# Gated mix of linear attention and a GEGLU MLP: changes of the moving side as own streams, values split when made, the first handover spread over two units

## The chip, the cores and the metric

The kernel runs on one core of one Trainium2 chip. The metric is the device time of one execution in microseconds (us). The kernel before takes 2434.32 us, the median of three runs (2431.76 to 2439.18).

## The reference

Two branches on the same tokens x (2048 x 1024) are mixed by a gate per token:

```python
g = sigmoid((x * gate_w).sum(-1, keepdims=True))
# a: hedgehog linear attention, 32 heads of 32
q, k, v = split(x @ wqkv)
phi(t) = concat(softmax(t @ w_phi), softmax(-(t @ w_phi)))     # per head
kv = einsum("bhsf,bhsd->bhfd", phi(k), v);  z = phi(k).sum over tokens
a = (phi(q) @ kv / (phi(q) @ z + 1e-6)) @ wo
# b: GEGLU MLP, 1024 -> 3584 -> 1024
b = (gelu(x @ w_gate) * (x @ w_up)) @ w_down
out = g * a + (1 - g) * b
```

## The kernel before

Every product is made in fp32 accuracy out of fp32r parts: each operand is split into a high part (a copy, by ScalarE, ACT) and a low part (a subtraction, by VectorE, DVE), and three passes (PASSES) of matmuls run for each pair. A 2x2 block product takes seven products instead of eight, of sums and differences of the blocks, which DVE makes. One such set is a **unit**: two row blocks of a weight matrix (the right operands x, y, z and v) against a quarter of a moving side (operands x and s). A unit has seven slots, and `product` (L680) issues twelve matmuls in each; `unit` ends and moves the banks of PSUM, and `results` passes the four result blocks on.

There are 79 units after the start: 1–7 for the values v, 8–15 for the keys k, 16–47 for queries q, gates g and ups u of one half of the tokens, and 48–79 for those of the other half (g and u alternate, the four q units stand between them). The first v unit is made plainly in the **start** (L267), straight from the raw wv and x blocks. w_phi is folded into the k weights by 16 **folds** (`fold_piece`, L287) right behind it and into the q weights by 16 more (L793). An out stage (L1369), which the change leaves alone, follows the last unit.

Where a group of units ends, the moving side changes (`change_half`): seven operands of four pieces are loaded by SyncE's DMA queue (SP), split by ACT and DVE and put into their place between the last use of the old and the first use of the new. This happens before unit 8 (the moving side becomes the folded k weights), unit 16 and unit 48 (the two halves of x).

Beside the units run: `key_sums` (sums of the folded k weights, stored for the first change), `gates` (the token gates), `features` (32 jobs: phi of a block of keys, split values, and the accumulation L913 into kv), `finish_z` (sums of phi over tokens) and `attention` (32 jobs: phi of queries, L1113, and the division). Results travel through DRAM: v and k rows by `store_rows`, queries, and the left operands la and lm of the out stage.

The order of all this is planned by hand when the kernel is built. Each helper is a generator that yields an earliest slot, a latest slot and its costs on DVE and ACT; `run_slot` picks, behind the twelve matmuls of each slot, those that are due or fit into the planned clocks of both engines. `fillers` are small groups of matmuls that are put behind a product. Each engine then works its own list strictly in that order, and so do the DMA queues of SP and of GpSimd (POOL), which carry loads and stores. The planner's numbers are fixed ones; what really takes longer makes the engine behind it wait.

Buffers set the rest: `stage` has three, `tyz` three (y and z of two units), `h` (`hidden`) three for results on their way out, `w0` four quarters (`gated`), `misc` two banks of PSUM.

The lines around the accumulation and the changes read:

```python
for h in range(2):
    high(vs[h][:, :, 0], pv[:, h])
yield now[0], NEVER, 0.75
for h in range(2):
    low(vs[h][:, :, 1], pv[:, h], vs[h][:, :, 0])
if after:
    load("v", work[:, 0], *after)
```

Of the kernel before, what the change touches and what calls it, by code (L numbers as in the profile page):

```python
# [16 lines left out]
P = 128  # L17
# [16 lines left out]
def tile_gated_mix(ctx: ExitStack, tc: tile.TileContext, x, xT, wkT, wqT, wv, w_phi, wo,  # L34
# [74 lines left out]
    tokens = {k: [dram.tile([NG, P, 4, P], F32, name=f"{k}t{b}") for b in range(S // BLK)] for k in "kv"}  # L109
# [44 lines left out]

    def store_chunk(m, i, k, t):
# [14 lines left out]
    with tc.manual_schedule(engines={PE, DVE, ACT, SP}):  # L170
# [22 lines left out]
        def plain_weights(s, n):  # L193
            k = kcs[s]
            for f in range(2):
                nc.scalar.dma_start(pieces[s // 4][:, s % 4:s % 4 + n, f * P:f * P + P],
                                    xT3[:, k:k + 4 * n - 3:4, f * BLK:f * BLK + P])
# [4 lines left out]
        nc.scalar.dma_start(phi_c, w_phi.rearrange("(g h) d f -> (h d) g f", h=4))  # L202
# [37 lines left out]
        for s in range(KC):  # L240
# [17 lines left out]
            if s == 3:  # L258
                for h in range(2):
                    t = fp.tile([P, 4, 4, 32], F32, tag=f"vs{h}", name="bp", bufs=1)  # L260
# [12 lines left out]
        rooms.append(new_work(0))  # L273
        homes = [t[:, n] for t, many in zip(rooms, (2, 2, 4)) for n in range(many)]
        homes.append(fa.tile([P, BLK], F32, tag="o2", name="fold", bufs=1))
        homes += homes[2:]
# [6 lines left out]
        def fold_piece(i):  # L283
# [7 lines left out]
            if 5 <= i < 12:  # L291
                fold_load(i + 4)

        for i in range(9):
            fold_load(i)
        results_0 = new_work(1)
# [9 lines left out]
        def plain_out(n, j, f):  # L306
            high(results_0[:, n], plain_banks[j, f])
            store_rows("v", 0, 1 - f, j, results_0[:, n])

        sum_steps(100)  # L310
        fold_piece(0)
        plain_out(0, 1, 0)
        fold_piece(1)
        plain_out(1, 0, 1)
        high(flat(x1)[0], first_e)
        low(flat(x1)[1], first_e, flat(x1)[0])
        fold_piece(2)
        plain_out(2, 0, 0)
        quarter_sums(first_e, first_o, True)
        high(flat(y1)[0], first_o)  # L320
        fold_piece(3)
        plain_out(3, 1, 1)
        low(flat(y1)[1], first_o, flat(y1)[0])
        x_splits = [(k, 0) for k in range(4)] + [(0, kc) for kc in range(1, 4)] + [(k, kc) for k in range(1, 4) for kc in range(1, 4)]
        x_highs, x_lows = zip(*[sum_parts(k, kc) for k, kc in x_splits])
        x_highs, x_lows = list(x_highs), list(x_lows)

        def more(n, m):
            for _ in range(n):
                x_highs.pop(0)()  # L330
            for _ in range(m):
                x_lows.pop(0)()

        more(2, 0)
        fold_piece(4)
        more(2, 4)
        fold_piece(5)
        more(3, 3)
        more_sums(first_e, first_o, True)
        z1 = slot()  # L340
        high(flat(z1)[0], first_e)
        fold_piece(6)
        low(flat(z1)[1], first_e, flat(z1)[0])
        more(9, 9)
# [69 lines left out]
        def key_sums(pa):  # L414
            for kc in range(KC // 2):
# [6 lines left out]
                for k in (kc - 1, kc):  # L422
                    r1, r2 = wide if k % 2 else [pa[:, 0], pa[:, 1]]
                    four = a11, a12, a21, a22 = r1[:, :BLK], r1[:, BLK:], r2[:, :BLK], r2[:, BLK:]
                    yield now[0], NEVER, 2.8
                    for _ in w_steps(*four):
                        pass
# [4 lines left out]
        def gates(pa):  # L432
            rows = [pa[:, 1], *wide]
            nc.sync.dma_start(pa[:, 0], gate_w[None, :].to_broadcast([P, D]))

            def load(c):
                nc.sync.dma_start(rows[c % 3], x[c * P:(c + 1) * P, :])
# [3 lines left out]
            for c in range(3):  # L441
                load(c)
            for c in range(S // P):
                r = rows[c % 3]
# [3 lines left out]
                if c + 3 < S // P:  # L448
                    load(c + 3)
# [6 lines left out]
        def change_half(t, half):  # L456

            b = 2 * half
            if half == 1:
# [8 lines left out]
            many = 2 if half == 3 else 1  # L468
            parts = [(i, j, t + free + 1, t + need) for i, free, need in order for j in range(0, 4, many)]
            if half < 3:  # L470
                homes = [gated(1, 0), *((gated(0, 0), gated(0, 1)) if half == 2 else (e2[:, 0], e2[:, 1]))]
            else:
                while not free[0]:
                    yield now[0] + 1, NEVER, 0.0
                free[0] = False
                raw = xa.tile([P, 2, 2 * BLK], F32, tag="pts", name="raw", bufs=1)
                homes = [raw[:, 0], raw[:, 1], *wide]
            N, H = len(parts), len(homes)
            TAIL = N if half < 3 else N - 6
            at = [n % H if n < TAIL else n % 2 for n in range(N)]  # L480

            def load(n):
                i, j, _, _ = parts[n]
                nc.sync.dma_start(homes[at[n]].rearrange("p (a b) -> p a b", a=many), srcs[i][:, j:j + many, :])

            loaded = [0]

            def more(n):
                while loaded[0] < N and (loaded[0] < H or any(at[m] == at[loaded[0]] for m in range(loaded[0] - H, n))):
                    if any(at[m] == at[loaded[0]] for m in range(n, loaded[0])):  # L490
                        break
                    load(loaded[0])
                    loaded[0] += 1

            def pieces(ns):
                for n in ns:
                    i, j, last, need = parts[n]
                    x = homes[at[n]].rearrange("p (a b) -> p a b", a=many)
                    yield max(now[0], last), need - 2, 0.0, 1.05 * many / 2
                    if j == 0 and i in (0, 3, 6):  # L500
                        q = ((b + 1, 0), (b + 1, 1), (b, 1))[i // 3]
                        xb[q] = new_quarter(*q)
                    q = [x_operands(half)[i][:, a, j:j + many, :] for a in range(2)]
                    high(q[0], x)
                    yield now[0], need - 1, 1.25 * many / 2
                    low(q[1], x, q[0])
                    more(n + 1)

            more(0)
            yield from pieces(range(TAIL))  # L510

            def tail():
                yield from pieces(range(TAIL, N))
                free[0] = True

            if TAIL < N:
                start(tail())
# [3 lines left out]
        for half in (2, 3):  # L521
            mine = [(half, k, m) for m in range(NF // 2) for k in "gu"]
# [7 lines left out]
        def weights(n, half, kind, m):  # L530
# [12 lines left out]
            if n == 1:  # L543
                mine.update(x=x1, y=y1, z=z1)
# [98 lines left out]
        gate_parts = []  # L643

        def gated(j, m):
            if not gate_parts:
                gate_parts.append(new_work(0))
# [15 lines left out]
        def plain_results(kind, half, m):  # L663
            def out(j, odd, x, t):
# [4 lines left out]
                else:  # L669
                    store_rows(kind, m, odd, j, t)  # L670
# [740 lines left out]
```

## Time and profile before

| what | us |
|---|---|
| median of three runs | 2434.32 (2431.76 to 2439.18) |
| the profiled execution | 2431.56 |
| its span | 2429.7 |
| TensorE (PE) busy | 2353.8 |
| DVE busy | 1759.0 |
| ACT busy | 1212.8 |
| GpSimd (POOL) busy | 364.5 |

In the trace a row of the timeline has the start, the duration, the engine, the line, the operation, the tiles (out<-in) with their shapes, and in brackets the idle time before it and what released it. ACTq and SPq are the engines' DMA queues. A row of a table by stretches has the stretch, its length, and for each engine the busy time with the count of instructions, then the granted TensorE clock (1.00 is full), the busy share of the DMA engines and the GB/s that they moved. A row of the waits has what waited and for what, the sum, the count and the longest. A row of DMA issues has the count, the size and the median time from issue to landing.

### The profile page before, as it was taken

The numbers are of one execution on the slowest core, as the hardware profiler recorded it, in microseconds if no ns is written. First come the engines' busy times: TensorE is split into PE (matmuls) and PEld (weight loads), VectorE is DVE, ScalarE is ACT, GpSimd is POOL, SyncE is SP. The second block draws the span as 40 slices with busy tenths as digits, with TensorE's granted clock in tenths as the row PEclk, the third lists the DMA queues.
The fourth block names the chain that finished last, engine by engine and source line by source line (L and its number), as shares of the span: only waits on it lengthen the run. The fifth ranks groups of instructions, "written<-read, shape, count | busy, mean of one in ns | idle before, by whom it ended". The sixth has DMA issues, their size and how long they took to land. (4 is left out here: it accounts for less than half of the span.)

```text
span 2429.7 us, 29400 instructions
## 1 busy us (share of the span) xinstructions
PE 2353.8 (97%) x10414; PEld 1931.5 (79%) x10414; DVE 1759.0 (72%) x2391; ACT 1212.8 (50%) x1706; POOL 364.5 (15%) x585
## 2 busy tenths in 40 slices
PE   7999999999999999999999899999999999999999
PEld 6777786788787777777778788888888888888887
DVE  6665456788987788856788788787375678877873
ACT  4335445565655555643777677777344222323221
POOL 1122331222221222211111111111000000000000
PEclk8999999999999999999999999999999999999999
DMA  7887678778887888897778778787786667887774
GB/s 244 277 269 254 231 247 277 281 280 299 298 286 259 285 270 285 278 358 281 234 244 266 230 252 270 244 262 242 248 302 216 234 216 267 311 288 280 269 272 139
DMA packets 243556, 640.70 MB, mean 264 GB/s; under 512 B 31680, under 2 KB 72400, under 8 KB 227024
## 3 DMA queue, kind: packets, MB, share of 16 engines
q1 hardware_dynamic: 183616, 428.14, 52.1%
q0 software_dynamic: 56544, 209.50, 25.2%
q8 instruction: 82, 1.34, 0.2%
q10 hardware_dynamic: 3248, 1.18, 0.2%
q14 instruction: 66, 0.54, 0.1%
HBM read 428.47 MB, written 210.51 MB: 263 GB/s over the span
## 5 line engine op out<-in xcount | busy, mean ns | idle before, releaser
L1369 PE MATMUL po<-tw,wgu 128*128 128x512 f32 x1344 | 309.8, 389 | 0.0
L56 ACT ACTIVATE wgu<-stage 128x1024 fp32r<-128x1024 f32 (+2 forms) x168 | 174.6, 1040 | 240.9 <-DVE stage L1259 160.8
L1369 PEld LDWEIGHTS po<-tw,wgu 128*128 128x128 f32 x1344 | 252.3, 188 | 52.4
L680 PE MATMUL b<-s,tyz 128*128 128x512 f32 x936 | 233.2, 397 | 13.9 <-ACT b L726 7.3
L680 PE MATMUL a<-s,tyz 128*128 128x512 f32 x948 | 233.8, 395 | 11.6 <-DMA tyz<-tu0z 3.7
L680 PE MATMUL p<-s,tyz 128*128 128x512 f32 x936 | 228.6, 393 | 8.6 <-DVE tyz L59 5.8
L680 PE MATMUL a<-s,v 128*128 128x512 f32 x948 | 232.9, 394 | 3.9 <-ACT s L56 3.1
L680 PE MATMUL a<-x,wgu 128*128 128x512 f32 x948 | 233.1, 395 | 2.8 <-DVE w L693 2.8
L59 DVE TENSOR_TENSOR wgu<-stage,wgu 128x1024 fp32r<-128x1024 f32 (+2 forms) x136 | 162.7, 1196 | 101.0 <-ACT wgu L56 100.0
L680 PE MATMUL c<-x,tyz 128*128 128x512 f32 x948 | 231.1, 392 | 2.3 <-ACT x L56 0.9
L680 PE MATMUL c<-x,wgu 128*128 128x512 f32 x948 | 230.0, 391 | 0.1
L680 PEld LDWEIGHTS b<-s,tyz 128*128 128x128 f32 x936 | 176.2, 190 | 58.2 <-ACT b L726 10.6
L680 PEld LDWEIGHTS a<-s,tyz 128*128 128x128 f32 x948 | 178.3, 190 | 52.9 <-issue 7.1
L680 PEld LDWEIGHTS p<-s,tyz 128*128 128x128 f32 x936 | 175.7, 189 | 49.7 <-DVE tyz L59 7.3
L680 PEld LDWEIGHTS a<-x,wgu 128*128 128x128 f32 x948 | 180.9, 192 | 42.5 <-DVE w L693 3.9
L680 PEld LDWEIGHTS a<-s,v 128*128 128x128 f32 x948 | 178.2, 190 | 43.0 <-ACT s L56 4.8
L680 PEld LDWEIGHTS c<-x,tyz 128*128 128x128 f32 x948 | 177.8, 189 | 41.9 <-ACT c L711 2.8
L680 PEld LDWEIGHTS c<-x,wgu 128*128 128x128 f32 x948 | 178.7, 189 | 38.0 <-DVE x L59 0.8
L56 ACT ACTIVATE tyz<-stage 128x1024 fp32r<-128x1024 f32 x95 | 100.2, 1055 | 120.8 <-DVE stage L134 118.4
L1369 PE MATMUL po<-tw,wl 128*128 128x512 f32 x672 | 156.9, 389 | 0.0
L1369 PE MATMUL po<-tyz,wgu 128*128 128x512 f32 x672 | 155.2, 389 | 0.0
L1369 PEld LDWEIGHTS po<-tw,wl 128*128 128x128 f32 x672 | 126.1, 188 | 26.2
(318 smaller groups left out, 3614.1 us busy)
## 6 DMA issues: line engine op xcount, KB each, us to landing
stage<-lm SPq DMA_DIRECT2D x98, 512.0 KB, 4.5
sr<-in_w_down SPq DMA_DIRECT2D x84, 512.0 KB, 5.0
sl<-lm SPq DMA_DIRECT2D x70, 512.0 KB, 4.8
lm<-h POOLq DMA_DIRECT2D x112, 256.0 KB, 5.8
stage<-in_w_gate SPq DMA_DIRECT2D x42, 512.0 KB, 7.1
stage<-in_w_up SPq DMA_DIRECT2D x42, 512.0 KB, 5.6
zs<-w POOLq DMA_DIRECT2D x32, 512.0 KB, 6.0
la<-h POOLq DMA_DIRECT2D x64, 256.0 KB, 5.4
```

What stands on the lines that cost most here:

```text
L56: nc.scalar.activation(dst, src, AF.Copy)
L59: nc.vector.tensor_tensor(dst, src, dst_h.bitcast(F32), OP.subtract)
L680: nc.tensor.matmul(dst, w[:, h, 4 * part + kc, :], xq[:, e, kc, :], start=first and kc == 0 and i == 0, stop=kc == 3 and i == 2, skip_grou ...
L1369: nc.tensor.matmul(ps[c], lefts[s][:, a, m, c * P:(c + 1) * P], made[k][:, e, m], start=d == 0 and m == 0 and n == 0, stop=d == n_duo - 1 ...
```

## The change

- **Start.** ACT issues one DMA of plain weights instead of ten and w_phi; the others, merged to seven, and w_phi go to POOL's queue.
- **Handover.** The first block sums of the v weights are made ahead of the raw sums; only two folds stand right behind the start, and the others, with the splits of the sums and the results of the plain unit, are spread over the slots of units 1 and 2.
- **Values.** v results are split into high and low parts when they are made (`split_values`) and stored with both parts (twice the bytes); a feature job loads them ready (`load_values`, one load of 512 KB behind the accumulation), so its two copies and two subtractions go. Three buffers take the splits in turn.
- **Changes of the moving side.** All three are streams of their own from 13 slots ahead, in 28 pieces of 256 KB through three spare buffers. Before, this held for the first two; the third ran inside the background stream in 14 pieces of 512 KB over four rooms.
- **Order.** q0 leads the first half and q1–q3 end it; q0–q3 lead the second half. Key sums run ahead of the gates, which use two buffers instead of three. Query folds start in slot 62 instead of 44 and use the masked w_phi without a copy.
- **z.** Row sums are transposed by the reduction itself; two transposes and two reductions go, one small reduction comes.

```diff
         def plain_weights(s, n):
...
+            for i in range(n):
+                (nc.gpsimd if s else nc.scalar).dma_start(dst[:, i], src[:, i])
...
+    def split_values(m, odd, j, i, dst, src):
...
+        nc.scalar.activation(d[:, :, 0], x, AF.Copy)
+        nc.vector.tensor_tensor(d[:, :, 1], x, d[:, :, 0].bitcast(F32), OP.subtract)
+        nc.gpsimd.dma_start(tokens["v"][b][g:g + 2, :, c].rearrange("g p f -> p g f"),
+                            dst.bitcast(F32).rearrange("p (g f) -> p g f", g=2))
...
+        value_homes = itertools.cycle((lambda: fp.tile([P, BLK], F32R, tag="qx", name="vh", bufs=1),
+                                       lambda: gated(0, 0).bitcast(F32R), lambda: gated(0, 1).bitcast(F32R)))
...
+        first_sums("y")
         sum_steps(100)
-        fold_piece(0)
-        plain_out(0, 1, 0)
...
-            many = 2 if half == 3 else 1
-            parts = [(i, j, t + free + 1, t + need) for i, free, need in order for j in range(0, 4, many)]
-            if half < 3:
-                homes = [gated(1, 0), *((gated(0, 0), gated(0, 1)) if half == 2 else (e2[:, 0], e2[:, 1]))]
-            else:
...
-                homes = [raw[:, 0], raw[:, 1], *wide]
...
+            parts = [(i, j, t + free + 1, t + need) for i, free, need in order for j in range(KC // 2)]
+            homes = [gated(1, 0), *((e2[:, 0], e2[:, 1]) if half == 1 else (gated(0, 0), gated(0, 1)))]
...
-            for m in range(N_Q):
-                mine.insert((0, 7, 12, 19)[m], (half, "q", m))
-            units += mine
+            lead = (1, N_Q)[half - 2]
+            units += [(half, "q", m) for m in range(lead)] + [(half, k, m) for m in range(NF // 2) for k in "gu"]
+            units += [(half, "q", m) for m in range(lead, N_Q)]
...
         def background(fjobs, jobs):
 
-            yield 9, NEVER, 0.0
+            yield 22, NEVER, 0.0
...
-            yield from gates(pa)
             yield from key_sums(pa)
             key_ready[0] = True
+            yield from gates(pa)
...
                     free[0] = True
+                    if after:
+                        load_values(*after)
...
-        between = [(7 * n - 13 + 3 * (units[n][0] == 3), change_half, (7 * n, units[n][0])) for n in TURNS]
...
+        for n in TURNS:
+            start(change_half(7 * n, units[n][0]))
...
+        extra = {
+            1: {0: [first_x, *folds(0, 2), outs[0], lambda: split_sums(0, kcs=range(4))],
+                1: [outs[1], *folds(2, 3)],
+                2: [outs[2], lambda: split_sums(1, 2, 3, kcs=(0,)), outs[3], lambda: first_sums("z"), lambda: split_sums(1),
+                    *folds(3, 5)],
...
+                6: folds(9, 11)},
+            2: {1: folds(11, 12), 2: folds(12, 13), 3: folds(13, 14), 4: folds(14, 15), 5: folds(15, 16)}}
```

The unit order also sets what each engine's list holds. On ACT, at the very beginning (stage holds the plain weights, phi_c is w_phi), there stood:

```order
L196 DMA stage<-in_xT 128x128 x4
L196 DMA stage<-in_xT 128x2x128 x6
L202 DMA phi_c<-in_w_phi 128x8x32
L56 ACT_TABLE_LOAD
L56 ACTIVATE wgu<-stage 128x256
```

and now there stands:

```order
L208 DMA stage<-in_xT 128x2x128
L56 ACT_TABLE_LOAD
L56 ACTIVATE wgu<-stage 128x256
L56 ACTIVATE x_376<-raw 128x512
L56 ACTIVATE wgu<-stage 128x256
```

Ten DMA issues have left ACT's list ahead of its first copy. At the handover, DVE's list now has the two sums of the first right operand and y's low part (first) ahead of ten of the raw sums (L146), and x's low part (wgu) behind them:

```order
L146 TENSOR_TENSOR raw<-raw 128x512
L133 TENSOR_TENSOR stage<-stage 128x512
L134 TENSOR_TENSOR stage<-stage 128x512
L59 TENSOR_TENSOR first<-stage,first 128x1024
L146 TENSOR_TENSOR raw<-raw 128x512 x6
L146 TENSOR_TENSOR raw<-h,raw 128x512
L146 TENSOR_TENSOR h<-h 128x512
L146 TENSOR_TENSOR h<-h,raw 128x512
L146 TENSOR_TENSOR h<-h 128x512
L59 TENSOR_TENSOR wgu<-stage,wgu 128x1024
```

Before, the raw sums came first there and the operand's parts behind them. On SP's queue at the third change (raw and w_670 the rooms, xs and in_xT the pieces' sources, tq0, tg0 and tu0 the saved right operands of units 48 to 50) there stood:

```order
L484 DMA raw<-xs_153 128x1024 x2
L541 DMA tyz<-tq0y 128x2048
L484 DMA w_670<-in_xT 128x2x512
L610 DMA o_8127<-in_w_up 128x512
L484 DMA w_670<-in_xT 128x2x512
L64 DMA stage<-in_w_gate 128x1024
L557 DMA wgu<-tg0x 128x1024
L484 DMA raw<-xs_154 128x1024
L541 DMA tyz<-tq0z 128x2048
```

and now there stands (w_543 holds the three rooms, vs the loaded values of a feature job):

```order
L480 DMA w_543<-xs_153 128x512 x4
L64 DMA stage<-wq_185 128x1024
L534 DMA wgu<-tq1x 128x1024
L480 DMA w_543<-in_xT 128x512
L518 DMA tyz<-tq0z 128x2048
L480 DMA w_543<-in_xT 128x512 x3
L600 DMA o_8150<-wq_184 128x512
L480 DMA w_543<-xs_154 128x512 x2
L518 DMA tyz<-tq1y 128x2048
L480 DMA w_543<-xs_154 128x512 x2
```

The pieces are twice as many and half as large, and the loads of the right operands stand between more of them.

More of the change, by code (lines that the diff above doesn't have):

```diff
@@ L486, in change_half @@
[L486 to L517, printed above, removed]
+                nc.sync.dma_start(homes[n % 3], srcs[i][:, j, :])
+            for n in range(3):
+                load(n)
+            for n, (i, j, last, need) in enumerate(parts):
+                x = homes[n % 3]
+                yield max(now[0], last), need - 2, 0.0, 0.6
+                if j == 0 and i in (0, 3, 6):
+                    q = ((b + 1, 0), (b + 1, 1), (b, 1))[i // 3]
+                    xb[q] = new_quarter(*q)
+                q = [x_operands(half)[i][:, a, j, :] for a in range(2)]
+                high(q[0], x)
+                yield now[0], need - 1, 0.7
+                low(q[1], x, q[0])
+                if n + 3 < len(parts):
+                    load(n + 3)
@@ L751, in unit @@
                     do()
-                run_slot(7 * n + k, 12 * (bool(before) or k not in (2, 4)) + fill + 4 * len(more_work),
+                run_slot(7 * n + k, 12 * (bool(before) or k not in (2, 4)) + fill + 4 * sum("folds" in do.__qualname__ for do in more_work),
                          0.7 * (k == 0), 0.6 * moved + 0.3 * (k == 0))
@@ L1026, in front, with attention @@
             box.append((key, s))
-        def attention(jobs, between):
+        def attention(jobs):
             job, box = jobs.pop(0)[1:], []
@@ L1042, in attention @@
                 key, raw = box.pop()
-                job = next_job(jobs, between)
+                job = next_job(jobs)
                 if job:
```

237 lines of the change are left out of this document (103 added, 134 removed).

## The prediction

> **What bounds the kernel now.** I read the engines' totals and the clock by slices first.
>
> ```profile
> span 2429.7 us, 29400 instructions
> PE 2353.8 (97%) x10414; PEld 1931.5 (79%) x10414; DVE 1759.0 (72%) x2391; ACT 1212.8 (50%) x1706; POOL 364.5 (15%) x585
> PEclk8999999999999999999999999999999999999999
> ```
>
> TensorE is busy 97% of the span, and the change leaves every one of its matmuls in place. So only three things can move: its idle time (2429.7 − 2353.8 = 75.9 us), stretches at half clock, and the order that causes both. The average hides where that sits, so I cut the span at the units' first matmuls (seven products of twelve matmuls; a unit starts with product a<-x,wgu) and asked for busy time and granted clock of each stretch.
>
> ```profile
> core 0: us, PE busy (x) PEld busy (x) DVE busy (x) ACT busy (x) POOL busy (x), PEclk, DMA share, GB/s
> 100.38:200.82 100.44, 96.95 (x422) 79.81 (x421) 68.48 (x114) 42.02 (x63) 26.67 (x40) 0.98 0.80 266
> 181.78:200.82 19.04, 19.04 (x86) 15.77 (x85) 13.27 (x19) 11.96 (x19) 5.96 (x8) 1.00 0.67 211
> 200.82:258.46 57.64, 50.94 (x209) 38.96 (x208) 28.14 (x40) 26.43 (x43) 14.05 (x20) 0.88 0.78 256
> 258.46:280.32 21.86, 21.86 (x111) 18.54 (x110) 8.92 (x11) 8.91 (x14) 8.12 (x12) 1.00 0.69 239
> 383.76:438.31 54.55, 47.25 (x170) 33.53 (x168) 28.73 (x41) 26.48 (x42) 8.05 (x14) 0.91 0.85 306
> 438.31:458.33 20.02, 20.02 (x94) 16.73 (x92) 16.93 (x24) 13.53 (x20) 4.55 (x8) 1.00 0.63 239
> 618.89:1024.29 405.40, 389.97 (x1766) 318.87 (x1765) 336.05 (x467) 235.76 (x343) 100.42 (x159) 1.00 0.84 280
> 1063.35:1132.52 69.17, 61.12 (x254) 49.33 (x253) 39.93 (x38) 22.74 (x33) 4.88 (x9) 0.95 0.85 315
> 1151.56:1371.85 220.29, 207.50 (x889) 167.22 (x888) 177.85 (x304) 154.94 (x228) 30.26 (x48) 0.98 0.76 242
> 1342.63:1371.85 29.22, 22.68 (x89) 17.89 (x88) 17.48 (x31) 15.01 (x24) 5.07 (x8) 0.88 0.65 198
> ```
>
> Unit 7 (second row) is an undisturbed one: 19.04 us, 84 matmuls at 0.227. Against that every stretch has an excess. Units 3–7: 100.44 − 5 × 19.05 = 5.2. Units 8–9, where the moving side changes the first time: 57.64 − 38.1, less five query folds of 0.9 (unit 10, the fourth row, holds three of them undisturbed: 21.86 − 19.05 = 2.8) = 15.0. Units 16–17, the second change: 54.55 − 38.1 = 16.4. Units 48–50, the third: 69.17 − 57.15 = 12.0. The inserted matmuls are counted by groups:
>
> ```profile
> L793 PE MATMUL misc<-w,fold 128*128 128x128 f32 x40 | 6.1, 303 | 0.0
> ...
> L913 PE MATMUL misc<-pts,vs 128*128 128x256 f32 x168 | 24.8, 292 | 5.8 <-DVE pts L59 5.8
> ...
> L1113 PE MATMUL misc<-pts,kbs 128*128 128x512 f32 x48 | 15.7, 431 | 9.8 <-ACT pts L56 7.0 <-DVE pts L59 2.8
> ```
>
> 40 of the first kind, eight to a fold, are the five folds of units 8–9. 168 of the second are 21 feature jobs, 0.97 us each (unit 18, 438.31 to 458.33, holds one and takes 20.02), so units 27–45 have 405.40 − 19 × 19.05 − 21 × 0.97 = 23.1 too much; 48 of the third are 12 attention jobs of 0.9, so units 52–61 have 220.29 − 190.5 − 10.8 = 19.0 too much. The path is PE all along; a term is what these excesses become.
>
> **Start and handover.**
>
> ```profile
> 0.74 6.37 ACTq L196 DMA_DIRECT2D stage<-in_xT  x10
> 10.58 0.79 PE L267 MATMUL c<-x,wgu 128*128 128x512 f32 x1 [5.67 <-ACT x L56]
> 19.07 0.62 ACT L56 ACTIVATE x<-raw 128x512 fp32r<-128x512 f32 x1
> 26.90 4.92 DVE L146 TENSOR_TENSOR raw<-raw 128x512 f32<-128x512 f32 x7
> 33.90 0.69 DVE L146 TENSOR_TENSOR h<-h 128x512 f32<-128x512 f32 x1
> 34.42 1.95 PE L287 MATMUL misc<-bp,stage 128*128 128x128 f32 x16
> 42.78 0.58 PE L287 MATMUL misc<-bp,w 128*128 128x128 f32 x1 [2.52 <-ACT fold L56]
> 51.73 1.59 PE L287 MATMUL misc<-bp,fold 128*128 128x128 f32 x8 [3.15 <-ACT w L56]
> 82.78 1.48 PE L680 MATMUL p<-s,tyz 128*128 128x512 f32 x3 [5.02 <-DVE tyz L59]
> ```
>
> ACT issues DMAs for 6.37 us before its first copy; now it issues one, and POOL, whose queue is empty then, the other seven and w_phi. The first matmul comes about 5.5 us earlier. What is late next is DVE: its last sum ends at 34.6. The low parts before the sums end at 26.9, and now not much before 23: the raw blocks land no earlier, ACT's last copy of one starts at 19.07, and five or six DVE instructions of 0.7 follow it. Then, in its new order, come two quarter sums (1.4), y's low part after ACT's copy (1.1 + 1.2), the ten sums (6.9, by the row of seven at 4.92) and x's low part (1.2): about 35. PE leaves the start stage at 28.8 (34.4 − 5.6), does two folds (1.8), and after two products' matmuls waits for that low part: some 5 us of stall. The other fourteen folds cost 0.9 each wherever they stand; where three stand in one slot, ACT must copy each out of one of two banks, and I allow 6 us in all, since the rows above show 2.52 and 3.15 for the same wait. Unit 3 then starts at 28.8 + 38.1 + 14.4 + 11 = 92.3 instead of 100.38: **−8**. Without any stall it is 81.3 (−19); with 82.78's wait left and new ones like it, 97 (−3).
>
> **Values split when made.** Per value unit eight half-width ACT copies, eight DVE subtractions and eight 256 KB stores of twice the bytes; per feature job two ACT and two DVE instructions leave.
>
> ```profile
> L56 ACT ACTIVATE vs<-w 128x256 fp32r<-128x256 f32 x60 | 21.4, 407 | 0.0
> L59 DVE TENSOR_TENSOR vs<-w,vs 128x256 fp32r<-128x256 f32 x60 | 22.6, 418 | 0.9 <-ACT vs L56 0.9
> SPq L851 <- DVE vs L59: 375.2, 29, 20.1
> vt<-h POOLq DMA_DIRECT2D x3, 256.0 KB, 5.5
> ```
>
> The busy time is 8 × 0.41 on each engine in a unit where DVE works 13.3 of 19 (the row of unit 7): hidden. The wait is not: the splits go round three buffers, each free only when its store has landed, 5.5 us by the last row; a buffer comes back one or two slots (2.7 us each) later, so ACT can stand before it, with the product copies behind it that PE needs. At 5.5 the slots about cover it. I take excess 5.2 → 8, **+3**, between −4 (the 3.5 us wait of unit 5, the gates' loads, goes, and nothing comes) and +15 (in each of five units 2 us of stall and 1 of clock). The key sums and the gates, whose loads stand in SP's queue there, only change places, and the query folds move one unit on, 0.9 each as before: 0.
>
> **Features.** SP's wait for DVE's subtraction (375 us in 440–1040 us) blocked the queue that also brings weights and right operands; the value load now follows the accumulation, needs no copy, and jobs stand one per unit, with no query unit among them. PE's waits there are for pts (5.8, above) and for ACT and DVE results behind those instructions; a wait near 3 us also costs clock:
>
> ```profile
> 875.39 1.86 PE L913 MATMUL misc<-pts,vs 128*128 128x256 f32 x7 [2.67 <-DVE pts L59]
> 875.00:877.00 2.00, 1.60 (x7) 1.61 (x8) 1.48 (x2) 0.44 (x1) 0.23 (x1) 0.50 1.06 421
> ```
>
> After that stall the granted clock is 0.50, which explains why the excess (23.1) is larger than the idle time (405.40 − 389.97 = 15.4). By the Trainium skill, TensorE: Matmul & The Clock Gate, section "What's actually happening", an idle window of about 3.4 us halves the clock, and the window runs free of the kernel; the trace agrees, with a stall of 2.67 enough here. The first clean units (20.02) show what a single job without a stall costs. I take 23.1 → 8, **−15**; bounds −20 (all but the pts waits gone) and −3 (DVE, 336 of 405 us busy, is the cause whatever SP does).
>
> **Third change of the moving side.** It had 14 loads of 512 KB over four rooms; it now has 28 of 256 KB over three, as the first two changes always had (these I leave at 15.0 and 16.4, ±4).
>
> ```profile
> w<-ks SPq DMA_DIRECT2D x10, 256.0 KB, 5.0
> raw<-xs SPq DMA_DIRECT2D x4, 512.0 KB, 7.9
> 208.55 1.26 ACT L56 ACTIVATE s<-w 128x512 fp32r<-128x512 f32 x2 [2.98 <-DMA w<-ks]
> 1119.95 1.43 PE L680 MATMUL a<-s,tyz 128*128 128x512 f32 x4 [3.70 <-DMA tyz<-tu0z]
> ```
>
> A room cycles in landing (5.0) + copy and subtraction (0.63 and 0.69) and some 0.7 in the engines' queues: 28 × 7.0 / 3 = 65 us, where the pieces may be taken only from slot −6 to +11, 17 × 2.72 = 46. The 19 us missing are about the 15–16 that the first two changes show, where ACT waits 2.98 for a piece. The third was spared that; its 12 come from z operands landing late (3.70 and two of 2.1–2.2, the waits of the same line). Those loads now stand in SP's queue behind pieces that wait for rooms. On the other hand the z-sum loads are gone from there. I take 16 + 4 = 20: **+8**, between −4 (pieces late nowhere, z as now less the z sums) and +23. By the Trainium skill, DMA: Bandwidth & Descriptors, section "Anatomy of one DMA — SWDGE (gpsimd) path", a transfer costs about 2.0 us and its bytes at 436 GB/s: 2.6 for a piece, an estimate, by which 28 × 4.6 / 3 = 43 fits into 46 and this term is −8, not +8. The measured 5.0 decides against it; the page's rule of batches of 1 MiB (section "Measured (HBM→SBUF, 128 partitions, SWDGE, issued from GpSimd)") speaks the same way as the row, against halving the loads.
>
> **Attention and z.**
>
> ```profile
> 1351.98 0.69 DVE L693 TENSOR_TENSOR h<-b,w 128x512 f32<-128x512 f32 x1 [5.94 <-DMA la<-h]
> 1354.30 0.79 PE L1113 MATMUL misc<-pts,kbs 128*128 128x512 f32 x1 [6.07 <-ACT pts L56]
> ```
>
> Here DVE stands 5.94 before an output buffer whose store is on its way, in a query unit, and PE 6.07 behind it. Query units now stand at the ends, outside this stretch. Unit 61, 1342.63 to 1371.85, is 29.22 − 19.05 − 0.9 = 9.3 too long by it. That goes, and the other 9.7 stay: **−9.5** (−14, if half of them goes as well, to 0, if the collision only moves to the units where queries now stand). z's eight reductions of 1.98 stay eight, and two transposes and two reductions leave; all of it lies beside PE: 0.
>
> Sum: −8 + 3 − 15 + 8 − 9.5 = −21.5. The profiled execution took 2431.56 (span 2429.7 and 1.9 around it), 2.8 below the median of 2434.32, so the forecast is 2431.6 − 21.5 = **2410**. The two sides of each term, added as squares, give 2396 to 2424 for this case.
>
> **The rivals.**
> *More of it* (2393): no DVE stall at the handover and the third change no worse than before, −9 and −8 more. For it: both were taken from worst-looking rows; against it: DVE's sums are only reordered.
> *The gains go back* (2431): the features stay at −3 and the collision of `h` buffers moves with the query units (0), 12 + 9.5 less. For it: DVE 83% busy between 619 and 1024; against it: clean units with the same work at 20.02.
> *Slower, by the piece stream at the third change* (2444): if a piece lands in 8 us, as the 512 KB pieces did there (7.9), 28 × 10 / 3 = 93 us stand against 46, 47 short instead of 20, and four waits over 3 us take about 1.7 each in clock (unit 61 lost 2.8 so: 9.3 of excess with 29.22 − 22.68 = 6.5 idle): +34, 2444. It makes the kernel slower by 0.3% from a landing of about 7.6 us. Against it: 5.0 for 256 KB under a similar load.
> That the change doesn't do what it says I give little: the value split and the loads stand in the order of instructions; only "spread over two" rests on waits.
>
> **How the numbers follow.** 0.60 for the forecast, 0.14 for more, 0.13 for 2431, 0.13 for slower. The range of 8 in 10 takes the forecast's own and reaches to the neighbours: 2389 to 2437. A measurement of this kernel tells 0.3% (7.3 us) from no change: faster means below 2427.0. That is 0.60 + 0.14 less the forecast's upper edge: 0.73; same 0.14; slower 0.13.
>
> **What would show it.** First matmul near 5; a PE stall for x's low part near 31–36; unit 3 at 89–97; no PE wait over 4 us in value units; the third change 16–24 us over its work with ACT waiting for pieces; units with one feature job mostly near 20.02; no wait for la or lm stores in DVE's rows. A wait of PE over 3 us in most value units, or a piece landing in 8, would make it wrong.

## The result and the profile after

The changed kernel takes 2455.46 us, the median of three runs (2454.77 to 2458.16), against 2434.32: a ratio of 1.0086 with a 95% interval of 1.0059 to 1.0114. It is 21 us slower than the kernel before; 2410 us were forecast. The engines' totals of the changed kernel:

```profile
span 2453.7 us, 29604 instructions
PE 2367.0 (96%) x10414; PEld 1939.4 (79%) x10414; DVE 1755.6 (72%) x2402; ACT 1212.1 (49%) x1702; POOL 393.7 (16%) x625
```

DVE and ACT are as busy as before; PE, with the same 10414 matmuls, is busy 13 us longer and idle 11 us longer (86.7 against 75.9). Longer busy time for the same matmuls is a lower clock: the mean granted clock of the profiled execution is 0.980, against 0.986 before. The stretches are cut at the first matmuls of units as before; a row has the stretch, its length, the busy times with counts by engine, and the granted clock behind them. Of the changed kernel these are, in order, units 3–7, unit 8 alone, units 8–9, 16–17, 18–26, 27–45, 47–51, 52–61 and 62–79:

```profile
97.81:209.79 111.98, 102.81 (x421) 80.59 (x419) 72.34 (x118) 43.81 (x81) 37.21 (x55) 0.95 0.81 277
209.79:251.32 41.53, 32.70 (x84) 19.99 (x85) 20.58 (x33) 16.54 (x32) 8.76 (x12) 0.75 0.69 228
209.79:279.97 70.18, 58.32 (x192) 40.17 (x193) 36.34 (x56) 30.17 (x54) 17.25 (x24) 0.81 0.70 230
407.07:463.73 56.66, 46.54 (x170) 32.37 (x168) 28.36 (x40) 25.22 (x39) 7.71 (x13) 0.94 0.77 277
463.73:648.54 184.81, 182.45 (x829) 151.64 (x828) 149.25 (x196) 108.06 (x144) 42.35 (x73) 0.99 0.84 293
648.54:1030.83 382.29, 381.64 (x1749) 317.21 (x1748) 312.42 (x407) 222.37 (x292) 95.25 (x153) 1.00 0.90 302
1050.85:1173.79 122.94, 105.68 (x438) 84.72 (x436) 56.04 (x79) 46.41 (x78) 22.72 (x38) 0.93 0.87 305
1173.79:1383.87 210.08, 204.17 (x890) 167.41 (x888) 177.75 (x301) 153.49 (x227) 26.87 (x43) 0.99 0.77 252
1383.87:1763.33 379.46, 371.80 (x1618) 306.09 (x1617) 289.50 (x483) 255.57 (x379) 50.20 (x79) 0.99 0.76 246
```

and of the kernel before, units 18–26, 47–51 and 62–79:

```profile
438.31:618.89 180.58, 180.47 (x830) 150.22 (x828) 150.79 (x208) 105.48 (x155) 42.08 (x74) 1.00 0.79 282
1044.31:1151.56 107.25, 99.20 (x422) 80.87 (x421) 60.58 (x65) 43.86 (x62) 13.31 (x24) 0.97 0.86 315
1371.85:1740.39 368.54, 368.44 (x1618) 302.50 (x1616) 283.70 (x470) 258.72 (x380) 49.28 (x78) 1.00 0.79 253
```

| stretch | before | after | difference | forecast of it |
|---|---|---|---|---|
| to unit 3 (start, handover) | 100.38 | 97.81 | −2.6 | −8 |
| units 3–7 (values) | 100.44 | 111.98 | +11.5 | +3 |
| units 8–9 (first change) | 57.64 | 70.18 | +12.5 | 0 |
| units 10–15 | 125.30 | 127.10 | +1.8 | 0 |
| units 16–17 (second change) | 54.55 | 56.66 | +2.1 | 0 |
| units 18–26 | 180.58 | 184.81 | +4.2 | 0 |
| units 27–45 (features) | 405.40 | 382.29 | −23.1 | −15 |
| units 47–51 (third change) | 107.25 | 122.94 | +15.7 | +8 |
| units 52–61 (attention) | 220.29 | 210.08 | −10.2 | −9.5 |
| units 62–79 | 368.54 | 379.46 | +10.9 | 0 |

They add up to +22.9, which is how much later the out stage begins (1763.33 against 1740.39). So three gains came, a small one at the start, a larger one than forecast on the features and the forecast one in units 52–61. Four losses of more than 10 us and three small ones took them back and more. Two feature jobs of 0.97 us, done in units 27–45 before, now stand in units 47–51 (438 matmuls recorded instead of 422), so 1.9 us in these two rows is work that moved.

### The profile page after: what moved, and what is told of

It is laid out like the page before. It is cut to its first block, busy times and chain, and to the rows that moved or that the text cites. A ratio compares the mean times of both kernels' runs of the same rounds, so it can differ in the third digit from the quotient of the medians.

```text
span 2453.7 us, 29604 instructions
## 1 busy us (share of the span) xinstructions
PE 2367.0 (96%) x10414; PEld 1939.4 (79%) x10414; DVE 1755.6 (72%) x2402; ACT 1212.1 (49%) x1702; POOL 393.7 (16%) x625
## 3 DMA queue, kind: packets, MB, share of 16 engines
q0 software_dynamic: 59488, 218.94, 25.7%
## 5 line engine op out<-in xcount | busy, mean ns | idle before, releaser
L665 PE MATMUL a<-s,tyz 128*128 128x512 f32 x948 | 243.1, 405 | 21.5 <-DMA tyz<-tq0z 5.9
L665 PE MATMUL c<-x,tyz 128*128 128x512 f32 x948 | 236.1, 398 | 18.0 <-ACT c L696 11.0
L665 PE MATMUL c<-x,wgu 128*128 128x512 f32 x948 | 235.1, 395 | 4.1 <-DVE x L59 2.4
L1343 PEld LDWEIGHTS po<-tyz,wgu 128*128 128x128 f32 x672 | 126.0, 188 | 27.0 <-DVE wgu L59 0.8
```

The source lines that it names most:

```text
L665: nc.tensor.matmul(dst, w[:, h, 4 * part + kc, :], xq[:, e, kc, :], start=first and kc == 0 and i == 0, stop=kc == 3 and i == 2, skip_grou ...
L1343: nc.tensor.matmul(ps[c], lefts[s][:, a, m, c * P:(c + 1) * P], made[k][:, e, m], start=d == 0 and m == 0 and n == 0, stop=d == n_duo - 1 ...
```

## The experiments

Single times of the kernel before scatter from 2423 to 2447 us over the runs below, so verdicts go by the stretches of each trace. Undisturbed units repeat there within 0.1 us. Disturbed stretches do not: units 16–17 took 56.5 to 62.3 us in the nine traces of the changed kernel and its variants in which nothing had been done about them. A difference of a few us in a disturbed stretch of one trace therefore shows little. Each experiment is one execution, but for e9 and e11, which ran six times.

### The value units and the first change

**e1_plain_values**

```diff
-            if kind == "v":
-                return lambda j, m: hidden() if m else None, out_parts
             return lambda j, m: hidden(), out
...
+                for h in range(2):
+                    high(vp[:, h, :, 0], pv[:, h])
+                yield now[0], NEVER, 0.75
+                for h in range(2):
+                    low(vp[:, h, :, 1], pv[:, h], vp[:, h, :, 0])
+                if after:
+                    load_values(*after)
...
                     free[0] = True
-                    if after:
-                        load_values(*after)
```

> The changed kernel with the value split undone alone: v results are stored plain, and each feature job splits its values itself, with the load behind the subtraction, as in the kernel before. Theory R (the three rooms of the value split hold ACT until a store has landed, and everything behind on ACT's list, the pieces of the first change too): units 3-7 go from 111.98 to 100-103 us, units 8-9 from 70.2 to 56-60. Theory G (the gates, which now run through the value units and into the first change, cause it): units 3-7 stay above 108 and units 8-9 above 66. For the features (units 27-45, 405.40 before, 382.29 in the changed kernel): if the split inside the job cost the time, they go back above 395; if the one-job-a-unit order did it, they stay below 388.

2421.63 us, beside 2435.98 for the kernel before on that chip. Its stretches (units 3–7, 8–9, 27–45 and 47–51):

```profile
98.21:193.41 95.20, 95.20 (x422) 78.85 (x420) 67.17 (x92) 38.87 (x58) 26.65 (x40) 1.00 0.88 297
193.41:250.29 56.88, 48.70 (x193) 36.73 (x192) 30.45 (x45) 25.72 (x41) 11.08 (x16) 0.91 0.76 253
617.49:1005.83 388.34, 383.99 (x1758) 317.78 (x1757) 324.57 (x451) 231.69 (x332) 95.72 (x154) 1.00 0.85 285
1024.89:1150.49 125.60, 107.93 (x446) 86.27 (x444) 54.50 (x81) 47.94 (x82) 22.24 (x36) 0.92 0.87 301
```

Units 3–7 are now five undisturbed units (5 × 19.05), 5 us better than the range that theory R gave. Units 8–9 lose 13.3 us, which is all of their growth. So the value split, in the kernel as changed, cost 16.8 and 13.3 us in these two places. The features, at 388.34, fall between the two expectations (above 395, below 388) and decide neither. The third change isn't helped by it (125.60 against 122.94).

**e2_late_gates**

```diff
             key_ready[0] = True
+            yield 66, NEVER, 0.0
             yield from gates(pa)
```

> The changed kernel with the gates' loads and DVE work held back until slot 66, behind the first change. Theory G: units 5-7 lose most of their excess (72.8 to about 62) and units 8-9 go from 70.2 to 56-60. Theory R: units 3-7 stay within 3 us of 111.98 and units 8-9 above 66.

The stream of the gates now begins in slot 66, in unit 9. Units 5–7 and 8–9 of this kernel:

```profile
135.26:198.88 63.62, 60.91 (x253) 48.79 (x252) 42.29 (x70) 29.31 (x55) 24.04 (x36) 0.95 0.75 251
198.88:261.50 62.62, 51.17 (x193) 36.17 (x192) 33.41 (x51) 28.62 (x50) 14.96 (x21) 0.89 0.81 260
```

Neither theory alone (2458.52 us): units 5–7 come down by 9.2 (72.8 to 63.6) and units 8–9 by 7.6. The two causes together cost more than the sum of each alone. In e1 the gates stand where the change put them, and units 5–7 are undisturbed beside them (57.1); the split without the gates costs 6.5 over that, and both together 15.7. In units 8–9 it is 5.7 and 13.3 over e1 (56.9); a kernel with neither was not run. The link is seen in ACT's waits for rooms and in the stores' landing, 137 to 250 us, first of the changed kernel, then of e2:

```profile
ACT w L160 <- DMA vt<-w: 12.4, 4, 4.7
ACT vh L160 <- DMA vt<-vh: 10.2, 4, 4.5
...
vt<-w POOLq DMA_DIRECT2D x20, 256.0 KB, 4.6
vt<-vh POOLq DMA_DIRECT2D x10, 256.0 KB, 4.1
```

```profile
ACT vh L160 <- DMA vt<-vh: 6.5, 3, 2.9
ACT w L160 <- DMA vt<-w: 5.4, 4, 2.9
...
vt<-w POOLq DMA_DIRECT2D x21, 256.0 KB, 3.4
vt<-vh POOLq DMA_DIRECT2D x11, 256.0 KB, 2.6
```

With the gates and their 512 KB loads there, a 256 KB store from `w` lands 1.2 us later at the median (4.6 against 3.4), and ACT stands 22.6 instead of 11.9 us before rooms. The feature jobs of e2 start later and stand more densely, about three to two units; its units 27–45 are taken up below.

**e5_four_rooms**

```diff
-                                       lambda: gated(0, 0).bitcast(F32R), lambda: gated(0, 1).bitcast(F32R)))
+                                       lambda: gated(0, 0).bitcast(F32R), lambda: gated(0, 1).bitcast(F32R),
+                                       lambda: hidden().bitcast(F32R)))
```

> The changed kernel, value split and all, with a fourth room for the split values (one of the h buffers) beside the three. Theory R: ACT's waits for vt stores between 137 and 250 us fall from 22.6 us to under 13, units 3-7 go from 111.98 to 103-108 us and units 8-9 from 70.2 to 60-66. Rival Q (what delays ACT is the order of its list, not the count of rooms, or the h buffer is as late as a room): less than 3 us in each.

2440.09 us. Units 3–7 and 8–9:

```profile
97.16:198.96 101.80, 96.74 (x422) 78.26 (x420) 72.25 (x118) 43.22 (x80) 36.66 (x55) 1.00 0.90 304
198.96:264.54 65.58, 52.80 (x192) 38.20 (x193) 36.40 (x56) 30.42 (x54) 17.52 (x25) 0.87 0.77 249
```

One room more, with the split, the gates and all else as changed, takes 10.2 of the 16.8 us and 4.6 of the 13.3. ACT waits 1.0 us in all for vt stores between 137 and 250 us, instead of 22.6, though a store landed no sooner (5.2 to 5.7 us at the median). Theory R holds for this part; Q falls. The other 6.6 and 8.7 us stay without any wait for a room: ACT now stands 12.3 us there for blocks loaded into `o`, where in e1 it stands 1.8. Whether the split's stores, of twice the bytes, delay these loads is not shown.

### The third change

**e3_z_on_pool**

```diff
-                load_parts("z", z)
+                (nc.gpsimd if 48 <= n < 53 else nc.sync).dma_start(z.rearrange("p a b c -> p (a b c)").bitcast(F32), sums[kind, m]["z"])
```

> The changed kernel with the loads of the z operands of units 48 to 52 issued from POOL's queue instead of SP's. PE waits 14.75 us in five waits for them. Theory S (they are issued late, since SP's queue stands before pieces that wait for their rooms): these waits fall below 4 us and units 47-51 go from 122.9 to 108-114. Rival L (issued late or not, a 1 MB load takes too long beside the other transfers): the waits stay above 10 us and the stretch within 3 us of 122.9.

Units 47–51 and PE's three largest waits there:

```profile
1052.21:1174.98 122.77, 107.98 (x437) 84.51 (x436) 54.23 (x77) 44.94 (x76) 20.01 (x34) 0.93 0.87 300
```

```profile
PE a L665 <- ACT c L709: 4.4, 1, 4.4
PE c L665 <- ACT x L56: 3.0, 1, 3.0
PE b L665 <- ACT s L56: 2.7, 1, 2.7
```

Half of theory S came true and its point did not: 1.1 us of the z waits are left, and the stretch is as long as it was, 122.77. With three rooms the wait for z only stood ahead of the pieces' own, and taking it away gains nothing. The whole took 2461.43 us; units 52–61 took 219.86 in it, against 210.08, and why stays open.

**e6_seven_rooms** (on e1)

```diff
+            if half == 3:
+                while not free[0]:
+                    yield now[0] + 1, NEVER, 0.0
+                free[0] = False
+                raw = xa.tile([P, 4, BLK], F32, tag="pts", name="raw", bufs=1)
+                homes += [raw[:, r] for r in range(4)]
+            H = len(homes)
```

> The kernel of e1 with seven rooms instead of three for the pieces of the third change (the four quarters of the pts tile beside the three, taken while no feature job accumulates). Theory P (28 pieces through three rooms take longer than the turn gives, and z operands, x and s parts are late in turn): units 47-51 go from 125.6 to 106-114 us. Rival L (the transfers themselves take too long then, whatever the rooms): above 120.

```profile
1027.92:1140.74 112.82, 102.77 (x446) 82.94 (x444) 54.43 (x78) 48.09 (x85) 18.05 (x28) 0.97 0.90 320
```

125.6 to 112.8, with 320 GB/s moved instead of 301: the transfers were not at their limit, the rooms were. Theory P holds. In the traces that follow, e7 to e11, the stretch stays at 111.1 to 113.6 with seven rooms; in the six with three it is 121.5 to 128.0. It is still longer than the 107.25 of before, and here z operands do come late (5.2 and 2.1 us of PE's waits): z loads from POOL's queue together with seven rooms were not run. The whole took 2417.26 us.

### The buffers of the attention

In units 54, 66 and 74 of the changed kernel the wait that the prediction saw in unit 61 is found again (units of 25.3, 26.4 and 25.7 us). POOL, DVE and PE in unit 66:

```profile
1465.01 0.56 POOL L130 DMA_DIRECT2D la<-h  x1 [6.63 <-ACT h L1075]
...
1472.98 0.87 POOL L130 DMA_DIRECT2D la<-h  x1 [6.50 <-DMA la<-h]
```

```profile
1472.65 0.69 DVE L678 TENSOR_TENSOR h<-b,w 128x512 f32<-128x512 f32 x1 [4.19 <-DMA la<-h]
```

```profile
1474.01 5.49 PE L665 MATMUL c<-x,tyz 128*128 128x512 f32 x12 [3.43 <-ACT c L696]
```

The second la store adds to what the first wrote, so it is issued only when the first has landed, 8 us later. Two of three `h` buffers are held all that time, and DVE, then ACT, then PE stand behind the third.

**e7_copies_apart** (on e6)

```diff
                     yield now[0] + 1, now[0] + 3, 0.0, 1.2
+                    while now[0] % 14 in (12, 13):
+                        yield now[0] + 1, now[0] + 3, 0.0, 1.2
                     hs = [hidden() for _ in range(2)]
```

> The kernel of e6 with the attention's copies out of PSUM kept out of the last two slots of u units, where they take two of the three h buffers just ahead of the subtraction that needs one. Theory H (buffers h held by la stores on their way stop DVE, then ACT and PE): the waits of DVE for la stores (two of over 3 us in e1) go and units 62-79 go from 375.1 to 369-371 us. Rival: they come up at other slots and units 62-79 stay within 2 us of 375.1.

Units 62–79, first of e6, then of e7:

```profile
1346.03:1725.82 379.79, 373.11 (x1626) 305.06 (x1624) 309.43 (x516) 271.58 (x401) 53.14 (x83) 1.00 0.79 249
```

```profile
1346.29:1718.00 371.71, 370.13 (x1625) 304.18 (x1624) 308.28 (x515) 270.86 (x401) 53.16 (x83) 1.00 0.80 255
```

8.1 us less than in e6, the kernel that differs by this edit alone; the expected 369 to 371 was missed by 0.7. DVE waits for no la store any more in e7 to e11; in e6 it waited 11.4 us for them in these units. Theory H holds for the wait. Its price is less sure than 8.1: less the units' and the attention jobs' own work (0.9 a job), the excess over these 18 units is 11.6 to 18.6 in six kernels without the edit (the changed one, e1 and e3 to e6), 7.7 to 9.2 in e7 to e10, and 7.6 before. So it is 2 to 11 us, from run to run. 2409.47 us, beside 2429.73 for the kernel before.

### The handover

**e4_x_first**

```diff
+        first_x()
         first_sums("y")
         sum_steps(100)
```

> The changed kernel with the high and low part of the first right operand's x made first on DVE and ACT, ahead of y's block sums and the raw sums, instead of behind them. Theory D (DVE's list is what PE waits 6.68 us for): that wait goes and unit 3 starts at 91-94 instead of 97.81. Rival N (the next work is late too: product p needs the sums and their splits): a wait of 4 us or more stands at p or at the folds instead, and unit 3 starts above 96.

Unit 3 starts at 97.80, as without the edit, and the whole takes 2454.65 us. PE's waits there, of the changed kernel and of e4:

```profile
PE a L665 <- DVE wgu L59: 6.7, 1, 6.7
PE misc L297 <- DMA fold<-in_wkT: 4.4, 1, 4.4
PE misc L297 <- DMA w<-in_wkT: 2.6, 1, 2.6
PE misc L297 <- ACT fold L56: 2.5, 1, 2.5
```

```profile
PE misc L297 <- DMA w<-in_wkT: 7.6, 2, 6.2
PE p L666 <- DVE s L59: 6.3, 1, 6.3
PE misc L297 <- DMA fold<-in_wkT: 3.3, 2, 2.0
```

Rival N holds: a wait of nearly the same length stands at the next product, and which of DVE's results PE meets first makes no difference to where unit 3 starts.

### Rooms at the other changes, and the features

**e8_five_rooms_first** (on e7) and **e9_rooms_at_all** (on e8). In both, the query folds that go through `w0` write over the last pieces of the first change, so the moving side of the k units is not the reference's; e10 mends that.

```diff
-            homes = [gated(1, 0), *((e2[:, 0], e2[:, 1]) if half == 1 else (gated(0, 0), gated(0, 1)))]
+            homes = [gated(1, 0), gated(0, 0), gated(0, 1), *((e2[:, 0], e2[:, 1]) if half == 1 else ())]
...
-            if half == 3:
+            if half > 1:
                 while not free[0]:
```

> The kernel of e7 with five rooms instead of three for the pieces of the first change (two quarters of w0 more, which are free there once the value split is gone). Theory P (three rooms are too few for 28 pieces): units 8-9, 58.3 us in e7, go to 45-52; what PE waits there for x and s parts falls below half. Rival L (transfers or the engines' copies set the pace): above 55.

> The kernel of e8 with seven rooms at the second change too (the pts tile, taken while no feature job accumulates). Theory P: units 16-17, 61.9 us in e7, go to 44-53, and the time to 2385-2400 us, the features and the attention unchanged within 5 us together. Rival L: units 16-17 above 57 and the time within 5 us of e8's.

In e8 units 8–9 take 53.95 (58.27 in e7), between the two expectations, and the whole 2404.92 us. In e9 the second change (units 16–17) all but vanishes, and the features get worse (units 27–45 in the second row):

```profile
369.53:408.94 39.41, 38.65 (x169) 31.38 (x168) 27.99 (x40) 24.91 (x40) 7.70 (x13) 1.00 0.97 369
590.98:1005.67 414.69, 393.49 (x1756) 317.14 (x1757) 330.50 (x459) 232.69 (x336) 97.99 (x157) 1.00 0.79 268
```

39.4 us are two units of 19.05 and 1.3; it was 61.88 in e7 and 61.23 in e8, and is 39.58 in e10. Theory P holds, more clearly than for the third change. But the features, expected unchanged, took the gain back: 414.69 against 389.23 in e7. So the whole, 2409.42 us over six runs, missed the expected 2385 to 2400.

**e10_rooms_mended**

```diff
             yield 62, NEVER, 0.0
+            while i and not taken[0]:
+                yield now[0] + 1, NEVER, 0.0
```

> The kernel of e9 with the query folds that go through w0 held back until the first change has taken its last piece. Expected as e9: units 8-9 at 50-54 us, units 16-17 at 38-42, units 27-45 at 408-418 with one feature job in each unit, split inside the job.

2398.8 us. Units 8–9 (first row) take 43.66 with one fold in them (177 matmuls recorded, 193 with three in e7): with five rooms to itself the first change costs 43.66 − 38.1 − 0.9 = 4.7, where e7 had 58.27 − 38.1 − 2.8 = 17.4. The expectation of 50 to 54 came from e9, where the folds still took two rooms away. Units 16–17, 39.58, came as expected. The features (second row) are as in e9:

```profile
192.13:235.79 43.66, 40.65 (x177) 32.10 (x176) 29.41 (x44) 24.09 (x40) 9.58 (x14) 1.00 0.91 303
...
585.59:1001.43 415.84, 394.75 (x1756) 318.56 (x1757) 330.47 (x459) 232.82 (x336) 98.03 (x157) 0.99 0.79 267
```

**e11_jobs_in_pairs** (on e10)

```diff
-                    fjobs += [(7 * (n + 1) + 6, m // 4, g, j) for g in (2 * i, 2 * i + 1) for j in range(2)]
+                    fjobs += [(7 * (n + 1) + 6 + 20, m // 4, g, j) for g in (2 * i, 2 * i + 1) for j in range(2)]
```

> The kernel of e10 with the feature jobs due 20 slots later, upon which the planner puts two into every other unit (the g units) instead of one into each, as in e1 and e7. Theory J (a job that splits its values itself does not fit beside every unit: before and e9 have one a unit and lose 23 to 26 us over 19 units, e1 and e7 two in every other and lose 7): units 27-45 go from 414.7 to 387-393 us and the time to 2380-2393 us. Rival K (the loss hangs on what else shifts there, loads and stores): units 27-45 stay above 405.

Units 27–45:

```profile
584.98:973.02 388.04, 383.70 (x1757) 317.94 (x1756) 324.49 (x451) 231.83 (x331) 94.71 (x154) 1.00 0.84 285
```

415.84 to 388.04, by when the jobs are due and nothing else. Less the units' and the jobs' own work, the excess over 19 units is 23.1 before and 33 in e9 (mostly one job a unit, split inside the job; the 23 to 26 in the expectation was too low for e9), 1.9 after (one a unit, split outside) and 7 to 8 in e1, e7 and e11 (two in every other unit, split inside). Theory J holds for jobs that split inside. But the split outside is no guarantee. Units 27–45 of e2 have it, with 22 jobs, one or two to a unit and none in the last three:

```profile
641.00:1045.14 404.14, 389.68 (x1773) 320.24 (x1772) 341.41 (x454) 228.26 (x306) 106.20 (x167) 1.00 0.92 304
```

Its excess is 404.14 − 361.95 − 22 × 0.97 = 20.9. The placing of the jobs counts in both forms. The price of e11's placing is further on: attention ends a unit later, units 52–61 take 212.01 (203.66 in e10) and units 62–79 382.09 (371.24), and PE waits 3.5 us at the start of the out stage.

Over six runs e11 takes 2391.79 us against 2433.87: a ratio of 0.983, interval 0.980 to 0.986. It is 42 us under the kernel before, and 64 us under the 2455.46 of the changed one. It is the change without its value split, with more rooms at all three changes, with the folds held back, the attention's copies kept apart and the feature jobs in pairs.

## Why the prediction was wrong

The terms were to add up to −21.5, and the span came out 24.0 longer. Half of the miss lies in two stretches that were put at nothing, the first change (+12.5) and units 62–79 (+10.9). The value units and the third change were each too small by about 8 us and the start by 5; the features gave 8 more than forecast.

**The step that failed first** is "as the first two changes always had (these I leave at 15.0 and 16.4, ±4)". The first change isn't edited much in its text, but it shares ACT's list with the splits of the last value units and SP's queue with the gates. Over its units' and folds' own work it takes 70.18 − 38.1 − 2.7 = 29.4 us instead of 15.0 (three folds stand in it now instead of five). e1 shows that 13.3 of it go with the split. An unedited stretch was taken for an unchanged one.

**Values: the mechanism was right, the size was not.** "At 5.5 the slots about cover it", +3; measured +11.5, inside the bound of +15. The landing taken was even too long (4.6 and 4.1). What was missed is the burst: six of a unit's eight splits stand close together. In e5, where ACT hardly waits for a room, the six of unit 3 start from 112.49 to 120.02 us, and the fourth 2.9 us after the first; with three rooms it needs the first one's room, while that store takes over 4 us to land. The gates, which now run behind the key sums, were costed at 0; without them a store from `w` lands 1.2 us sooner (e2). Of the excess of 16.7 in units 3–7 only 9.2 is idle time, with no wait over 2.3 us; the rest is slow matmuls. So the sign that was to show this term wrong, waits over 3 us in most value units, never came.

**Clock.** In unit 8 the longest wait is 2.23 and the idle time 41.53 − 32.70 = 8.8, but the unit is 22.5 us too long: the granted clock is 0.75 over the whole unit, and the rest, 13.7, is slow matmuls. The prediction counted half-clock time only behind waits near 3 us, but for 1 us a unit in its bound for the values; its own row had a halved clock behind a wait of 2.67. That wait is shorter than the 3.4 us set beside it, so the trace bears out the halving there, not the length.

**Third change: right, and too small.** +8 was forecast for units 48–50; +15.7 came over units 47–51, of which 1.9 are the two feature jobs. The sum by rooms (28 pieces, three rooms, 65 us against 46) named the cause that e6 shows. That z operands would be late was what PE met first; without that wait the stretch was no shorter (e3). The rival on this place did not happen: pieces landed in 4.0 us (x sums) and 6.7 (x itself) at the median there, not in 8, and not in the 2.6 of the estimate set against the sum. The same sum also held for the second change, where seven rooms took 22 us off (e9, e10).

**Features: more gain, and not for the reason given.** That SP's wait for DVE's subtraction "blocked the queue" falls as a cause. SP's waits between 440 and 1040 us, first before, then after (in e1 it is 340.8):

```profile
SPq L851 <- DVE vs L59: 375.2, 29, 20.1
```

```profile
SPq L828 <- PE misc L881: 396.6, 28, 16.0
```

SP waited longer after than before, while the excess went from 23.1 to 1.9. That a bigger gain came than forecast is thus in part luck. What the runs show is narrower: at one job a unit, the excess is 23 to 33 with the split inside the job and 1.9 with it outside; in e11 the pairing with g units alone takes a job that splits inside to 6.7; and in e2 jobs without a split, placed unevenly, lose 20.9.

**Attention.** The wait in unit 61 went, and units 52–61 gave 10.2, as forecast. But the collision moved to units 54, 66 and 74, and units 62–79, put at 0, gave 10.9 back. The prediction had this as the far end of its bound ("to the units where queries now stand"), at the wrong place: it came where the copies met a u unit's last slots (e7). The 10.9 is in part the luck of one trace: the five other kernels without e7's edit had 4.4 to 11.3 there.

**Start and handover.** The first matmul at 5.26 and the wait for x's low part (6.68 against "some 5") came. The folds' waits sum to 9.5 instead of 6, and 7.0 of that are loads of folds, which the sum had not; unit 3 at 97.81, against 92.3, is just outside the range of 89 to 97.

**The range.** "The two sides of each term, added as squares" do not give 2396 to 2424. With the bounds as stated they give about −19 and +25 around 2410, 2391 to 2435. The measured 2455 lies outside that too.

What stays open: what the split still costs with four rooms (6.6 and 8.7 us in e5); why single runs of one kernel differ in units 16–17 (58.9 in e1, 62.3 in e6, the same program up to there); and the 4.2 us of units 18–26, where the trace of the changed kernel has one unit with two jobs and a wait of 2.36.

## What to carry to other kernels

A store moved earlier makes its buffer's life as long as the store's landing: count how many such buffers are wanted within one landing time in the worst few slots, not on average, and what stands behind the waiting instruction in its list. Count the rooms of a stream the same way, pieces × (landing + work) / rooms against the time of the window, since four rooms more were worth 22 us at one change here. The landing in this sum is not fixed: with seven rooms at the third change a piece of x sums landed in about 8 us at the median, with three in 5.3, and the change was still 12.8 us shorter (e6 against e1). And weigh edits by every stretch that shares a list, a queue or a buffer with them, not by the stretches that the diff names.

## What the runs showed of the hardware

In unit 8 of the changed kernel, with several waits of 0.2 to 2.3 us close together, the granted clock was 0.75 over 41.5 us; each of these waits was shorter than the 2.67 behind which it stood at 0.50 in the kernel before. A store of 256 KB from `w` landed in 3.4 us at the median in e2, and in 4.6 in the changed kernel, where 512 KB loads of the gates ran beside it. Both are at a mean of 249 to 259 GB/s, below the 369 and 384 moved at the second change in e9 and e11, so a landing can grow while the transfers are far from the most that was seen. SP's queue waited 397 us in 600 for the accumulations of the changed kernel, and the 19 feature units beside it lost 1.9 us in all.
